# Transposing x by DMA instead of on TensorE, and accumulating two output projections in one PSUM bank

## The chip, the cores and the metric

The kernel runs on one core of one Trainium2 chip. The metric is the device time of one execution in microseconds (us). PE is TensorE (PEld its weight loads), DVE is VectorE, ACT is ScalarE, POOL is GpSimd, SP is the engine that issues the DMAs.

## The reference, cut to what matters

A gated mix of an attention block with a compressive memory (A) and a feed-forward block (B), both on the same 2048 x 512 input x, in bf16:

```python
g = sigmoid((x * gate_w).sum(-1, keepdims=True))      # one gate per row
a = A(x)     # q, k, v projections; 32 heads of 16; 4 segments of 512 rows:
             #   causal softmax attention inside the segment,
             #   plus phi(q) @ M / (phi(q) @ z) from earlier segments; then @ wo
b = (relu(x @ W_gate) * (x @ W_up)) @ W_down          # hidden size 1792
return g * a + (1 - g) * b
```

## The kernel before

The program is a list of tasks for each engine. A small list scheduler in the kernel's own Python, with a duration estimated for each task, puts them in a fixed order per engine and adds semaphore waits. So every edit that changes a dependency or an estimated duration can rebuild the order of all engines.

x is loaded in row layout, transposed on PE (64 transposes of 128 x 128) and copied out of PSUM by DVE:

```python
for c in range(NCH):                       # 4 chunks of 512 rows, loaded into E[c]
    for kt in range(KT):                   # 4
        def f_tr(pe, ...):
            for tt in range(TT):
                pe.transpose(PLb[:, bank, col:col + 128], E[:, e, tt, kt * 128:(kt + 1) * 128], ident[:])
        def f_cp(dv, ...):
            return dv.tensor_copy(xT[:, kt, c * 512:(c + 1) * 512], PLb[:, bank, 0:512])
```

The set-up on GpSimd, in this order: `ident`, `mumask`, memset of `vaug` (4352 bf16 per partition), two small memsets, memset of `wkp` (4096 bf16), then eight strided copies from `wk` into `wkp`. The loads are issued in the order x chunk 0, wq, gate_w, wk, wv, beta, x chunks 1 to 3, then the feed-forward weights.

The output stage of a segment, for each of its four tiles of 128 rows:

```python
# down projection of the hidden tile hT (14 matmuls), evicted by DVE
f_ob: psA  = sum_f hT[f].T @ wd[f]
tmpB:  tmpB = psA * (1 - g) + 0                  # DVE, 512 columns
# attention projection (4 matmuls), evicted by DVE
f_oa: psA' = sum_G oT[G].T @ wo[G]
fin:   osb  = psA' * g + tmpB                    # DVE, 512 columns; then the store
```

The softmax here doesn't subtract the row's maximum and nothing guards it: scores larger than these inputs give would overflow.

## Time and profile before

Median 367.0 us of 4 runs. The engine table of the page of the kernel before (busy us, share of the span, number of instructions):

```profile
## 1 busy us (share of the span) xinstructions
PE 323.3 (88%) x3039; PEld 181.1 (50%) x3072; DVE 230.1 (63%) x581; ACT 216.5 (59%) x275; POOL 94.8 (26%) x149
```

Next, the kernel before by windows. Columns: the stretch, its length, then busy us of each engine with the number of instructions, the mean granted clock of PE (1.00 is full), the DMA share and rate.

```profile
core 0: us, PE busy (x) PEld busy (x) DVE busy (x) ACT busy (x) POOL busy (x), PEclk, DMA share, GB/s
0.00:12.19 12.19, 1.89 (x16) 1.66 (x17) 4.36 (x10) 1.69 (x3) 10.85 (x17) 1.00 0.73 241
...
30.00:60.00 30.00, 25.64 (x256) 10.60 (x258) 24.57 (x59) 22.35 (x24) 9.07 (x14) 0.94 0.23 74
60.00:278.00 218.00, 196.21 (x1980) 99.82 (x2001) 146.82 (x387) 162.49 (x185) 72.05 (x112) 1.00 0.02 6
278.00:345.80 67.80, 66.89 (x563) 52.44 (x564) 34.70 (x79) 21.46 (x56) 0.63 (x1) 1.00 0.03 11
345.80:366.00 20.20, 15.61 (x70) 6.78 (x70) 6.45 (x10) 0.38 (x1) 0.00 (x0) 1.00 0.08 26
```

The attention runs until 278 us with feed-forward matmuls as filler; PE is 90% busy there. (Between 30 and 60 us the clock was 0.94: this run had one stretch at half clock, from 55.34.) From 278 the rest of the feed-forward runs alone and PE is practically full. Before 12.19 us PE does 1.9 us of work. So the kernel is bound by PE's work plus a late start.

The start, in lines of the timeline of the kernel before (start, duration, engine, line, operation, output and inputs, count; in brackets the idle time before and what ended it):

```profile
2.52 3.72 POOL L525 MEMSET vaug<- 128x4352 bf16 x1
...
4.90 1.49 DVE L574 COPY xT<-psL 128x512 bf16<-128x512 bf16 x3 [1.19 <-PE psL L570]
...
11.41 0.31 DVE L540 CAST beta_i<-beta_raw 128x32 f32<-128x32 bf16 x1 [5.02 <-DMA beta_raw<-in_A_beta_dram]
11.63 0.41 DVE L574 COPY xT<-psL 128x512 bf16<-128x512 bf16 x1
...
12.19 3.57 PE L614 MATMUL psA<-xT,wq 128*128 128x512 bf16 x8 [6.05 <-DVE xT L574]
...
25.27 0.40 PE L730 MATMUL psL<-qT,kp 32*128 32x512 bf16 x4
```

DVE copies three of the first four transposed tiles, then stands 5 us for the beta load, then does the fourth; the first projection (L614) follows. The first score matmul (L730) comes at 25.27, after the other transposes.

In the output stage, PE and its weight loads wait for the eviction of the down projection (list of waits; total us, number, longest):

```profile
PEld psA L856 <- DVE tmpB L824: 3.2, 7, 1.3
...
PE psA L856 <- DVE tmpB L824: 1.5, 3, 0.8
```

### The profile page before, as it was taken

How to read it: one execution, taken by the hardware profiler on the slowest of the kernel's cores; microseconds unless marked ns; L12 is line 12 of the kernel's file. 1: busy time of each engine (PE TensorE's matmuls, PEld its weight loads, DVE VectorE, ACT ScalarE, POOL GpSimd, SP SyncE). 2: the span in 40 equal slices, each digit the busy share in tenths (PEclk: the TensorE clock that was granted, in tenths of full speed). 3: DMA queues.
4: the chain of work that ended last, by engine and by line, in shares of the span. 5: the costliest groups of instructions: out<-in, count | busy, mean ns of one | idle time of the engine just before them, and what ended most of it. 6: DMA issues, size and time to landing. Idle time of an engine off the chain costs nothing.

```text
span 365.5 us, 7442 instructions
## 1 busy us (share of the span) xinstructions
PE 323.3 (88%) x3039; PEld 181.1 (50%) x3072; DVE 230.1 (63%) x581; ACT 216.5 (59%) x275; POOL 94.8 (26%) x149
## 2 busy tenths in 40 slices
PE   2698978898899998898899898888998999999995
PEld 1353333354454454443334455555345886488842
DVE  4484898977876656789955548944346543464433
ACT  1337786578887788865665789788554441034400
POOL 8402233233333333333322333333322000000000
PEclk9999998999999999999999999999999999999999
DMA  6960240000000000000000000000000000100001
GB/s 216 365 240 22 69 157 2 0 4 0 2 2 2 0 2 2 3 0 16 0 29 17 1 3 2 1 2 2 14 16 29 3 2 0 36 23 2 3 14 43
DMA packets 10113, 12.27 MB, mean 34 GB/s; under 512 B 1120, under 2 KB 9056, under 8 KB 10080
## 3 DMA queue, kind: packets, MB, share of 16 engines
q1 hardware_dynamic: 10080, 11.81, 9.4%
q8 instruction: 24, 0.39, 0.5%
q14 instruction: 9, 0.07, 0.1%
HBM read 9.71 MB, written 2.10 MB: 32 GB/s over the span
## 4 chain that ended last, share of the span: by engine, by line
PE 60%; DVE 19%; ACT 13%; issue 3%; DMA 2%; SPq 1%; POOL 1%; DVEq 0%; ACTq 0%
PE psA L820 12%; PE psA L788 11%; ACT E L736 11%; PE psA L793 10%; PE psL L730 6%; PE psA L627 5%; PE psA L636 3%; PE psA L749 3%; PE psA L856 3%; DVE amem L687 3%; DMA beta_raw<-in_A_beta_dram 2%; PE psA L614 2%; PE psA L647 2%; DVE kp L630 2%; PE psA L763 1%
## 5 line engine op out<-in xcount | busy, mean ns | idle before, releaser
L736 ACT ACTIVATE E<-psL 128x2048 bf16<-128x2048 f32 (+3 forms) x128 | 158.1, 1235 | 57.0 <-PE psL L730 55.7
L738 POOL TENSOR_SCALAR_AFFINE_SELECT E<-E 128x512 bf16<-128x512 bf16 x128 | 82.4, 644 | 182.7 <-ACT E L736 182.5
L800 DVE TENSOR_TENSOR hT<-psA,rl 128x256 bf16<-128x256 f32 x112 | 47.1, 422 | 51.3 <-ACT rl L799 50.9
L799 ACT ACTIVATE rl<-psA 128x256 bf16<-128x256 f32 x112 | 42.8, 382 | 51.3 <-PE psA L793 27.9
L788 PE MATMUL psA<-xT,wg 128*128 128x256 bf16 x448 | 67.5, 273 | 0.6 <-DMA wg<-in_B_W_gate_dram 0.4
L793 PE MATMUL psA<-xT,wu 128*128 128x256 bf16 x448 | 67.4, 273 | 0.0
L730 PE MATMUL psL<-qT,kp 32*128 32x256 bf16 (+3 forms) x512 | 40.4, 305 | 14.0 <-ACT E L736 13.2
L820 PE MATMUL psA<-wd,hT 128*128 128x512 bf16 x216 | 51.1, 379 | 0.5 <-issue 0.2
L788 PEld LDWEIGHTS psA<-xT,wg 128*128 128x128 bf16 x448 | 40.8, 98 | 10.5 <-issue 2.4
L793 PEld LDWEIGHTS psA<-xT,wu 128*128 128x128 bf16 x448 | 41.9, 98 | 7.8 <-issue 1.0
L730 PEld LDWEIGHTS psL<-qT,kp 32*128 32x128 bf16 x512 | 12.9, 91 | 50.8 <-ACT E L736 38.6
L820 PEld LDWEIGHTS psA<-wd,hT 128*128 128x128 bf16 x224 | 21.0, 98 | 24.1 <-issue 0.8
L627 PE MATMUL psA<-xT,wkp 128*128 128x512 bf16 x120 | 31.4, 391 | 1.4 <-issue 0.9
L757 DVE CAST pvT<-psA 128x512 bf16<-128x512 f32 x32 | 22.0, 688 | 12.7 <-PE psA L749 12.7
L630 DVE CAST kp<-psA 128x512 bf16<-128x512 f32 x32 | 22.0, 687 | 7.9 <-PE psA L627 7.4
L749 PE MATMUL psA<-E,vaug 128*17 128x256 bf16 (+3 forms) x512 | 23.1, 300 | 1.7 <-POOL E L738 0.8
L824 DVE SCALAR_TENSOR_TENSOR tmpB<-psA,omg_all,zero 128x512 bf16<-128x512 f32 x16 | 12.0, 750 | 18.8 <-PE psA L820 18.8
L614 PE MATMUL psA<-xT,wq 128*128 128x512 bf16 x59 | 17.0, 419 | 7.0 <-DVE xT L574 6.0
L861 DVE SCALAR_TENSOR_TENSOR osb<-psA,g_all,tmpB 128x512 bf16<-128x512 f32 x16 | 12.0, 750 | 17.0 <-PE psA L856 17.0
L749 PEld LDWEIGHTS psA<-E,vaug 128*17 128x17 bf16 x512 | 10.2, 89 | 15.5 <-issue 5.1
L856 PE MATMUL psA<-wo,oT 128*128 128x512 bf16 x60 | 15.6, 380 | 2.5 <-DVE tmpB L824 1.5
L627 PEld LDWEIGHTS psA<-xT,wkp 128*128 128x128 bf16 x128 | 11.1, 100 | 13.1 <-issue 2.9
(68 smaller groups left out, 276.8 us busy)
## 6 DMA issues: line engine op xcount, KB each, us to landing
E<-in_A_x_dram SPq DMA_DIRECT2D x4, 512.0 KB
out_dram<-osb SPq DMA_DIRECT2D x16, 128.0 KB
wg<-in_B_W_gate_dram SPq DMA_DIRECT2D x1, 1792.0 KB
wu<-in_B_W_up_dram SPq DMA_DIRECT2D x1, 1792.0 KB
wd<-in_B_W_down_dram SPq DMA_DIRECT2D x1, 1792.0 KB
wq<-in_A_wq_dram SPq DMA_DIRECT2D x1, 512.0 KB
wk<-in_A_wk_dram SPq DMA_DIRECT2D x1, 512.0 KB
wv<-in_A_wv_dram SPq DMA_DIRECT2D x1, 512.0 KB
```

Of the source, the lines that this page charges most:

```text
L627: ins = pe.matmul(A(ep)[:, :], lhsT=wkp[:, kt, n, :], rhs=xT[:, kt, tok0:tok0 + 512], start=(kt == 0), stop=(kt == KT - 1))
L630: dve_t.append(Tk("dve", lambda dv, n=n, ep=ep: dv.tensor_copy(kp16[:, s2, n, :], A(ep)[:, :]), writes=[f"kp16_{s2}_{n}"], dur=c_dve(512), ...
L730: ins = pe.matmul(PL[:, jj, 0:N], lhsT=kp16[32 * jj:32 * jj + 32, s2, n, 128 * j:128 * j + 128], rhs=qT16[32 * jj:32 * jj + 32, s2, G, 128 ...
L736: act_t.append(Tk("act", lambda ac, e=e, N=N: ac.activation(E[:, e, :, 0:N], PL[:, :, 0:N], ACT.Exp, scale=SCALE), reads=[f"bankL{q4}" for ...
L738: pool_t.append(Tk("pool", lambda pl, e=e: pl.affine_select(out=E[:, e, :, 0:128], in_=E[:, e, :, 0:128], compare_op=ALU.is_ge, fill=0.0, ...
L749: ins = pe.matmul(A(epv)[32 * jj:32 * jj + 17, 128 * j:512], lhsT=vaug[:, s2, j, h, :], rhs=E[:, es[j], jj, 0:N], start=(j == 0), stop=(j ...
L788: ins = pe.matmul(A(ep)[:, 0:256], lhsT=wg[:, kt, f * 128:(f + 1) * 128], rhs=xT[:, kt, t0:t0 + 256], start=(kt == 0), stop=(kt == KT - 1))
L793: ins = pe.matmul(A(ep)[:, 256:512], lhsT=wu[:, kt, f * 128:(f + 1) * 128], rhs=xT[:, kt, t0:t0 + 256], start=(kt == 0), stop=(kt == KT - 1))
L799: act_t.append(Tk("act", lambda ac, ep=ep, r=r: ac.activation(rl[:, r, :], A(ep)[:, 0:256], ACT.Relu), writes=[f"rl{r}"], dur=c_act(256), ...
L800: dve_t.append(Tk("dve", lambda dv, ep=ep, r=r, f=f, half=half: dv.tensor_tensor(hT[:, f, half * 256:(half + 1) * 256], A(ep)[:, 256:512], ...
L820: ins = pe.matmul(A(ep)[:, :], lhsT=hT[:, f, i * 128:(i + 1) * 128], rhs=wd[:, f, :], start=(f == 0), stop=(f == NF - 1))
L856: ins = pe.matmul(A(ep)[:, :], lhsT=oT[:, G, i * 128:(i + 1) * 128], rhs=wo[:, G, :], start=(G == 0), stop=(G == 3))
```

## The change

Its intent: take the transposes off PE and the copies off DVE by loading x with transposing DMAs, start earlier, and save the tmpB evictions by letting the two output projections accumulate into one bank. With z the gate's logit, g = e^z (1 - g). So the attention rows are multiplied by e^z where they are normalised anyway, the down projection accumulates on top, and one eviction multiplies the sum by (1 - g).

The core of the diff (renamings, the same dependency per tile in many places, a dependency of every first matmul on the clearing of the PSUM banks, and a longer estimate for the load of wu are cut):

```diff
-            self.now[e] = start + 700.0
+            spb = 1300.0 if task.name.startswith("ldxT") else 700.0      # scheduler's estimate of an issue
+            self.now[e] = start + spb
...
+    def xT_dmas(c):
+        for kt in range(KT):
+            srcx = A_x[0, c * 512:(c + 1) * 512, kt * 128:(kt + 1) * 128]
+            dma(lambda sp, ...: sp.dma_start_transpose(xT[:, kt, c * 512:(c + 1) * 512], srcx), writes=[f"xT{c}_{kt}"], ...)
+    # order of loads: beta, wq, wk, x chunk 0 (4 transposes), gate_w, wv, x chunks 1-3 (12), wg, wu, wo, wd
...
     pool_setup: ident
+                wkp memset, 8 wkp copies, vaug memset          # moved up
                 mumask, zero32, zero512
-                (before: mumask, vaug memset, zero32, zero512, wkp memset, 8 wkp copies)
...
-    (64 PE transposes xtr{c}_{kt} and 16 DVE copies xcp{c}_{kt})
...
-    g_all = sigmoid(z);  omg_all = 1 - g_all
+    omg_all = sigmoid(-z);  gexp = exp(z)
...
-    amem = num * rec                        # tensor_tensor
+    amem = (num * gexp) * rec               # scalar_tensor_tensor
+    rdg  = rden * gexp                      # 32 small multiplies
-    adot = pv * rden
+    adot = pv * rdg
...
+            pe_out.append(Tk("pe", f_oa, reads=[oT..., "wo"] + [f"hT{f}" for f in range(NF)], ...))   # 4 matmuls, stop=False
+            (f_ob: 14 matmuls onto the same bank, start=False, in two halves of 7)
-            tmpB = psA * omg_all;   osb = psA' * g_all + tmpB
+            osb  = psA * omg_all
```

## The prediction

> **What bounds the kernel now.** The engine table of the page: PE 323.3 of 365.5 us (88%), DVE 230, ACT 217; clock 0.995. The chain of waits is 60% PE. By windows, PE's 42 us of idle lie in four places: 10.3 us before the first projection starts at 12.19; some 27 us scattered through the attention part (30 to 280); 0.2 from 280 to 350, where the feed-forward part runs back to back; 4.6 after. So: PE-bound, with a late start.
>
> The start, from the timeline: the 64 PE transposes of x take about 6.9 us of PE (16 take 1.7 in the chain), all before 25 us, with 16 DVE copies of 416 ns (6.5 us). After three of the first four copies (6.4 us) DVE stands for the beta load, issued late (3.48, landed 11.39); the fourth copy, hence the first projection, comes only at 12.0. The first score matmul runs at 25.3.
>
> **What the change does.**
> 1. x arrives transposed by 16 DMAs of 128 KB. PE loses 6.9 us of work, DVE 6.5.
> 2. Beta, wq and wk go first, so that DVE stall is gone; but the first projection needs four transposing DMAs. Plain issues take 0.44 to 0.89 us of the SP queue; the diff's scheduler charges 1.3 us for a transpose. Three issues (1.9 us) plus four at 1.3, from 0.8, end near 7.9; with about 2 us to land I estimate the first projection at 10 to 11. The Trainium skill ("DMA: Bandwidth & Descriptors", section "Latency and other measured facts") gives 261 GB/s for a DMA transpose with a non-contiguous middle dimension: an estimate of 2 us for the first 512 KB, 8 us for all x, less than the issuing (16 x 1.3 = 21 us). No trace shows one yet.
> 3. wg and wu land about 10 us later (wg lands at 20.4 now). Almost no feed-forward runs before 60 us, so this should cost nothing.
> 4. The down projection accumulates onto the attention projection in one PSUM bank. 16 tmpB evictions (750 ns, 12.0 us) leave DVE, and PE's waits for them (4.7 us) go. Added on DVE: 32 small multiplies (16-column ones take 160 to 250 ns: about 7 us) and perhaps 60 ns on each of 48 amem operations (3 us). The first output matmul of a segment now waits for the last hT: about 1.2 us of idle, which at the end eats the saved tmpB step.
>
> **On the critical path.** Transposes 6.9 us and the start 1 to 2 us count nearly in full: attention starts near 16 us instead of 25 and the rest slides forward. The DVE saving is off the path except for 2 to 3 us. The end is a wash. Together 10 to 11 us: **356 us, 349 to 364**. Faster by over 2%: 0.70; within 2%: 0.23; slower: 0.07.
>
> **Signs.** Right: no PE transposes of x in the groups; first projection at 10 to 11 us, first score matmul at 15 to 18; PE busy near 317, DVE near 222; no waits for tmpB; attention ending near 270, then about 85 us of dense feed-forward. Wrong: first projection later than 13 us, or PE standing for a DMA in the gate matmul (which needs all of x) or the first feed-forward block.
>
> **What would make it wrong.** Transposes far slower than 1.3 us each; the rebuilt order filling the attention part better or worse by several us; the added DVE step in the attention chain, where DVE is 95% busy (40 to 60 us).

## The result, and the profile after

Median 359.9 us of 10 runs (359.63 to 361.4) against 366.9 us of 16 runs of the kernel before. The ratio is 0.9822, 95% interval 0.9803 to 0.984: faster by 1.8%, so within 2%. Here and below, a ratio is the mean time of one kernel's runs over that of the other's of the same rounds, so it is not quite the ratio of the medians quoted. Executions over 1.5% slower than the fastest of the same kernel are left out of the means. The time lies in the stated range, but the predicted gain was 10.9 us (366.9 - 356.0) and the measured one is 7.0, and the forecast that had been given 0.70, faster by over 2%, did not come true.

The engine table of the page of the kernel after:

```profile
PE 317.8 (88%) x2974; PEld 175.8 (49%) x3008; DVE 224.0 (62%) x580; ACT 216.0 (60%) x276; POOL 94.3 (26%) x149
```

PE lost 5.5 us of busy time and DVE 6.1, as expected. The windows of the kernel after, cut at the same events:

```profile
0.00:9.28 9.28, 0.00 (x0) 0.03 (x1) 4.28 (x9) 3.03 (x4) 6.10 (x12) 1.00 0.68 171
9.28:30.00 20.72, 18.30 (x81) 6.79 (x83) 14.94 (x31) 8.60 (x9) 8.89 (x14) 0.92 0.67 175
...
60.00:272.40 212.40, 192.44 (x1941) 98.32 (x1967) 143.93 (x387) 159.46 (x182) 69.82 (x110) 0.99 0.03 8
272.40:340.00 67.60, 65.59 (x546) 51.08 (x546) 30.46 (x71) 21.46 (x56) 0.94 (x2) 1.00 0.03 11
```

Two things differ from what was forecast. The clock is lower: 0.92 in the second stretch and 0.99 in the attention part, where the profile before had one dip, 0.94 between 30 and 60 us. And the dense part, where PE was 0.9 us short of full before, is now 2.0 us short (67.60 - 65.59).

The start in the timeline of the kernel after:

```profile
2.26 5.11 SPq L498 DMA_TRANSPOSE xT<-in_A_x_dram  x4
...
9.28 4.90 PE L604 MATMUL psA<-xT,wq 128*128 128x512 bf16 x16 [9.28 <-DMA xT<-in_A_x_dram]
...
10.65 3.72 POOL L534 MEMSET vaug<- 128x4352 bf16 x1
...
11.91 2.76 DVE L610 TENSOR_SCALAR ttmp<-qT 128x512 bf16<-128x512 bf16 x1
...
18.45 0.39 PE L720 MATMUL psL<-qT,kp 32*128 32x512 bf16 x4 [2.09 <-DVE kp L620]
```

The four transposing DMAs take 1.28 us each to issue (5.11 / 4), and the first projection starts at 9.28 us, even earlier than predicted. But the first tensor_scalar on DVE takes 2.76 us; the same operation takes 0.28 later. It ends 0.3 us after the GpSimd memset of vaug does (10.65 + 3.72 = 14.37; 11.91 + 2.76 = 14.67). Everything behind it on DVE is late, PE stands, and the first score matmul comes at 18.45 instead of 15 to 18.

In the output stage the waits for tmpB are gone and new ones are there (waits of PE, kernel after):

```profile
PE psA L827 <- DVE hT L793: 2.6, 2, 1.3
...
PE psA L827 <- DVE mutmp L698: 1.0, 1, 1.0
...
PE psA L827 <- DVE rden L758: 0.3, 1, 0.3
```

L827 is the first output matmul of a segment: it waits for all hidden tiles, twice 1.3 us in front of the dense output stages, and in the attention part for a DVE count that stands behind other DVE work (mutmp, rden).

Finally the clock. The trace's clock records show stretches of exactly 3.41 us at half clock: in the profiled run of the kernel after two of them, from 18.74 and from 148.45. Windows of the kernel after around them:

```profile
145.00:148.45 3.45, 1.59 (x43) 0.83 (x40) 2.14 (x6) 2.09 (x4) 1.76 (x3) 1.00 0.00 0
148.45:151.86 3.41, 3.41 (x41) 1.43 (x41) 1.47 (x3) 1.88 (x1) 0.63 (x1) 0.50 0.01 2
15.00:18.74 3.74, 1.37 (x9) 0.41 (x8) 3.64 (x11) 1.89 (x3) 0.89 (x3) 1.00 0.46 105
18.74:22.15 3.41, 3.41 (x12) 1.19 (x9) 1.96 (x10) 1.88 (x1) 0.65 (x1) 0.50 0.49 112
```

In front of both PE had been busy for less than half the time (1.59 of 3.45 us, 1.37 of 3.74). The Trainium skill ("TensorE: Matmul & The Clock Gate", section "Part 1: The HAM clock gate") describes a gate that halves PE's clock after an idle window, with a window of 3413 ns that runs freely. The length agrees with the records here. But PE was not idle in front of these stretches, and its busy time does not decide either. The profiled run of e4 (below) went to half clock right after this window, with PE busy for 2.72 of 3.41 us, 1.74 of them 64 one-column matmuls of the gate:

```profile
17.90:21.31 3.41, 2.72 (x70) 2.03 (x71) 2.55 (x6) 1.32 (x2) 0.00 (x0) 1.00 1.03 406
```

In e8 and e3, windows with 1.75 and 1.84 us of 3.41 busy (from 17.49 and from 143.82) were followed by none. What sets off a stretch is not settled here.

The clock column needs a caution too: it reads 1.00 also where the trace has no clock record. The first record begins at 17.79 us in the profiled run before and at 11.92 in that after. Until then PE ran at about half clock, as its instructions show: the weight loads of the first projection start 0.43 us apart (before: 12.57, 13.00, 13.42, 13.85), later 0.21 (after: nine in 1.89 us from 11.79). From the first projection on that is 5.6 us before and 2.6 after, so an estimate from these spans is that it cost the run before 1.5 us more (half of the difference). The first record falls elsewhere in other profiled runs (12.37 in e1, 15.26 in e5), so whether the change has a part in it is not shown.

Such a stretch costs time, and the number of them differs from run to run of one kernel. It shows in the granted clock listed with every run: 1.0 or 0.999 for none, 0.994 or 0.995 for one, 0.990 or 0.991 for two (read from the traces where there is one). The runs by that grade:

| kernel | none | one | two |
|---|---|---|---|
| before (rounds of e1 to e4) | 365.6 to 366.5, 9 runs | 367.9, 368.3 | - |
| after | - | 359.6 to 359.9, 7 runs | 361.2 to 361.4, 4 runs |
| e1 | 356.0 to 356.6, 4 runs | 358.7 | 359.9 |
| e2 | 354.8 to 355.3, 5 runs | 356.7 | - |
| e3 | 358.8 | 360.2 to 360.5, 4 runs | 361.9 |
| e5 | 352.8 to 353.4, 4 runs | 355.5, 355.6 | - |

(Two runs of before at 0.997, of which no trace is kept, are counted with none by their times.) One stretch costs 1.2 to 2.5 us between the medians of neighbouring columns, and comparisons finer than that are made below within one column, though some columns hold a single run. Over all rounds before has eleven runs at 0.995 (367.2 to 368.3, median 367.6). Against the seven of after with one stretch the gain is 7.8 us, where the medians of all runs give 7.0.

### The profile page after: what moved, and what is told of

It is laid out like the page before. It is cut to its first block, busy times and chain, and to the rows that moved or that the text cites. A ratio compares the mean times of both kernels' runs of the same rounds, so it can differ in the third digit from the quotient of the medians.

```text
span 359.5 us, 7318 instructions
## 1 busy us (share of the span) xinstructions
PE 317.8 (88%) x2974; PEld 175.8 (49%) x3008; DVE 224.0 (62%) x580; ACT 216.0 (60%) x276; POOL 94.3 (26%) x149
## 4 chain that ended last, share of the span: by engine, by line
PE 53%; DVE 23%; ACT 16%; issue 4%; SPq 1%; DMA 1%; POOL 0%; DVEq 0%; ACTq 0%
PE psA L835 14%; ACT E L726 10%; PE psL L720 7%; PE psA L781 7%; DVE hT L793 6%; ACT rl L792 5%; PE psA L617 5%; PE psA L786 4%; PE psA L739 4%; PE psA L626 4%; PE psA L827 3%; DVE amem L677 3%; DVE kp L620 2%; DVE qT L608 2%; PE psA L753 2%
## 5 line engine op out<-in xcount | busy, mean ns | idle before, releaser
L781 PE MATMUL psA<-xT,wg 128*128 128x256 bf16 x448 | 67.5, 273 | 0.1
L781 PEld LDWEIGHTS psA<-xT,wg 128*128 128x128 bf16 x448 | 41.0, 98 | 10.4 <-issue 2.7
L839 DVE SCALAR_TENSOR_TENSOR osb<-psA,omg_all,zero 128x512 bf16<-128x512 f32 x16 | 12.0, 748 | 35.1 <-PE psA L835 35.1
L617 PE MATMUL psA<-xT,wkp 128*128 128x512 bf16 x120 | 32.3, 397 | 1.7 <-DVE amem L677 0.7
L604 PE MATMUL psA<-xT,wq 128*128 128x512 bf16 x60 | 16.1, 405 | 9.9 <-DMA xT<-in_A_x_dram 9.3
L827 PE MATMUL psA<-wo,oT 128*128 128x512 bf16 x59 | 15.4, 379 | 4.0 <-DVE hT L793 2.6
L677 DVE SCALAR_TENSOR_TENSOR amem<-psA,gexp,ndrec 128x128 bf16<-128x128 f32 x48 | 16.5, 345 | 1.3
```

What stands on the lines that cost most here:

```text
L617: ins = pe.matmul(A(ep)[:, :], lhsT=wkp[:, kt, n, :], rhs=xT[:, kt, tok0:tok0 + 512], start=(kt == 0), stop=(kt == KT - 1))
L677: dve_t.append(Tk("dve", lambda dv, dst=dst, srcn=srcn, bc=bc, t=t: dv.scalar_tensor_tensor(out=dst, in0=srcn(), scalar=gexp[:, t:t + 1], ...
L781: ins = pe.matmul(A(ep)[:, 0:256], lhsT=wg[:, kt, f * 128:(f + 1) * 128], rhs=xT[:, kt, t0:t0 + 256], start=(kt == 0), stop=(kt == KT - 1))
```

## The experiments

All give a correct result. Each was timed in five rounds beside the kernel before on the same chip (six runs each, but five of e6 and four of e8). Differences to the 359.9 us of the kernel after are those of the medians. Taken through the ratios to before (0.9822 for after) they are smaller: 2.5 us for e1, 4.7 for e2, 5.8 for e5.

### e1: the memset of vaug earlier

Theory: the GpSimd memset keeps DVE's first operation on SBUF operands from running. The Trainium skill ("SBUF — State Buffer", section "Who interferes with whom") says that DVE and GpSimd share a pair of SBUF ports under an exclusive lock, that copies, casts and tensor_scalar can take it on the DVE side, and that a DVE operation with at most one SBUF input, outside the modes that use two ports, does not contend. The copies from PSUM in the kernel before agree (413 to 425 ns beside the memset). The edit keeps the order of PE, DVE and ACT the same as after's (compared instruction by instruction), so nothing but the memset's place differs:

```diff
     pool_setup: wkp memset
+                vaug memset (all of it)         # here POOL waits for wk anyway
                 8 wkp copies
-                vaug memset
+                memset of one element of vaug   # keeps the dependencies and the order
```

> The kernel after, with the 3.7 us GpSimd memset of vaug moved ahead of the wkp copies (a one-element memset keeps its old place, so that the order of PE, DVE and ACT is the same as after's). Theory A (that memset holds the SBUF ports that the first DVE tensor_scalar needs): the first tensor_scalar drops from 2.76 us to under 0.8, the first score matmul comes at 15.5 to 16.5 us instead of 18.45, and the total falls by 2 to 4 us, to 356 to 358. Rival B (the late start is given back in the attention part): the first score matmul comes earlier, but the total stays within 1 us of 359.9. Rival C (the long tensor_scalar has another cause): it stays near 2.7 us.

Measured: 356.4 us (6 runs, 356.0 to 359.9), ratio 0.9755 (0.9715 to 0.9794). Two lines of its timeline:

```profile
11.88 0.67 DVE L611 TENSOR_SCALAR ttmp<-qT 128x512 bf16<-128x512 bf16 x1
...
16.51 0.39 PE L721 MATMUL psL<-qT,kp 32*128 32x512 bf16 x4 [0.40 <-DVE kp L621]
```

The tensor_scalar fell from 2.76 to 0.67 us (the small wkp copies still run beside it) and the first score matmul moved from 18.45 to 16.51. Theory A held. The hold is moved, not gone: the memset now lies beside the beta cast, which took 4.87 us (1.19 in after) and ended at 8.68 as the memset did (8.64). There it costs nothing, as DVE then waits for the first projection until 11.15. Of the 3.5 us, only 1.1 to 1.4 are seen between runs with equally many half-clock stretches (358.7 against 359.8; 359.9 against 361.3; one run of e1 each). The rest is that four of six runs had no such stretch, where all eleven of the kernel after had one or two. That is consistent with the profiled run, in which one of them followed directly on the stall (15.00 to 18.74 above), but what decides which run gets one is not settled; that part is argued, not shown.

### e2: no wait for the last hidden tile

Again the same order on all engines. Only the semaphore wait of the first output matmuls on the last hidden tile is left out; they don't read it. The second half of the down projection, which does, keeps its wait.

```diff
+            pe_out[-1].soft = (f"hmul{s}_{NF - 1}_0", f"hmul{s}_{NF - 1}_1")   # ordered after, not waited for
```

> The kernel after in the same order on every engine; only the first output matmul group of a segment no longer waits for the last hidden tile (the second half of the down projection still does, where it is read). Theory A (the two 1.3 us PE waits before the output stage of segments 2 and 3 lie on the path): both vanish and the total falls by 2.3 to 2.9 us, to about 357.3. Rival: the wait only moves to the second half of the down projection, and the total stays within 0.7 us of 359.9.

Measured: 354.95 us (6 runs, 354.8 to 356.7), ratio 0.9694 (0.9669 to 0.972). More than expected. In its timeline the output stage follows without a gap (no bracket):

```profile
294.20 0.81 PE L830 MATMUL psA<-wo,oT 128*128 128x512 bf16 x3
```

Its list of PE's waits has none of the three lines shown for after, so 2.6 + 1.0 + 0.3 = 3.9 us of waits are gone; the expectation had counted only 2.6, the two in the dense part. In runs with one half-clock stretch the difference to after is 3.1 us (356.7, a single run, against 359.8). The rest is again the number of stretches: five of six runs had none. In the kernel after, the wait of 1.0 us lies at 146.7 to 147.8 us, inside the thin stretch before the half clock at 148.45; in the profiled run of e2, PE was busy 2.36 and 3.00 of 3.40 us in the two stretches there, and no half clock followed.

### e3: DVE's saved work put back

```diff
+                if t < 12:      # segments 0 to 2: one more 512-column eviction, to a scratch tile
+                    dv.scalar_tensor_tensor(out=scr[:, t, :], in0=A(ep)[:, :], scalar=omg_all[:, t:t + 1], in1=zero512[:, :], ...)
                 return dv.scalar_tensor_tensor(out=osb[:, r, :], ...)
```

> The kernel after with 12 extra 512-column DVE evictions of 0.75 us (9 us of DVE work), one beside each output eviction of segments 0 to 2, the order otherwise the same. It puts back the load that dropping tmpB took off DVE, without its waits. Theory A (that saving lies off the path): total within 1 us of 359.9. Rival (DVE time in the attention part counts, as the prediction's 2 to 3 us assumed): 3 us or more longer.

Measured: 360.25 us, ratio 0.9832 (0.9803 to 0.986), 0.4 us more than after, and 0.4 us too within the column of one stretch. Nine us of DVE work more cost almost nothing. The DVE time that dropping tmpB saves lies off the critical path.

### e4 and e11: the kernel before with beta issued first

e4 moves one load. e11 adds that the two memsets write the same bytes as fp32, half as many elements, in the same order as e4.

```diff
# e4
+    dma(beta_raw <- A_beta)            # first of all
     for c in range(NCH): ...
-            dma(beta_raw <- A_beta)    # before: sixth
# e11, on top
-    pl.memset(wkp[:], 0.0)
+    pl.memset(wkp[:].bitcast(F32), 0.0)
-    pl.memset(vaug[:], 0.0)
+    pl.memset(vaug_flat[:].bitcast(F32), 0.0)
```

> The kernel before with one edit: the beta load is issued first. Theory A (the start of before is bound by DVE standing for beta): the first projection starts at 7 to 8.5 us instead of 12.19 and the total falls by 2 to 4.5 us, to 362.5 to 365. Rival (the 12.19 is bound by the loads of x or wq): first projection stays later than 10 us and the total within 1 us of 366.9.

> e4 (the kernel before with beta issued first) with the two memsets written as fp32, in the same order as e4. Theory A (in e4 the beta cast on DVE was held for 6.5 us by the two memsets): the cast falls to under 2 us, the first projection comes 3 to 5 us earlier than e4's 18.1, and the total falls by 2 to 4 us to 360 to 362. Rival (e4's start is bound by the other three loads of x, which its order puts first): the cast is short but the first projection stays later than 17, total within 1 us of 364.3.

Measured: e4 364.3 us, ratio 0.9948 (0.9923 to 0.9973); e11 364.1 us, ratio 0.9944. Both expectations failed in part, and e4 shows why its own did. From its timeline:

```profile
2.52 3.72 POOL L525 MEMSET vaug<- 128x4352 bf16 x1
3.75 6.50 DVE L540 CAST beta_i<-beta_raw 128x32 f32<-128x32 bf16 x1
...
6.71 3.51 POOL L528 MEMSET wkp<- 128x4096 bf16 x1
```

Beta was there at 3.75, but the cast of 32 columns took 6.50 us, until 10.25: it was held through the memset of vaug, two small ones, and that of wkp, which ended at 10.22. Removing the wait for the load had only uncovered a second one. In e11 the cast takes 2.98 us and ends at 6.74, again as the (shorter) memset of wkp ends (6.71). So the hold is real. Yet the first projection stays at 17.6 us against 18.1 in e4, and the total does not move, as the rival said: the rebuilt order puts all 64 transposes in front of the first projection, so the loads of the later chunks set its time (PE stands 5.45 us for one until 12.60). Both runs together show that the reordered load by itself, with the order rebuilt around it, was worth 2 us.

### e5 and e9: both mends

e5 is e1 and e2 together, e9 adds the fp32 memsets; both in the same order as after on PE, DVE and ACT.

> The kernel after with both mends of the first two runs (vaug memset early, no wait for the last hidden tile), in the same order on PE, DVE and ACT. If the two are separate waits, their gains add: 359.9 - 3.5 - 4.9 = 351.5 us; part of each may be the same half-clock window, counted twice, so 351 to 353.5. If they hide each other: 355 or more.

> Both mends (as e5), and the two long GpSimd memsets (wkp, vaug) write the same bytes as fp32, half the elements; the order on PE, DVE and ACT is the same as after's. If a memset costs per element, each falls from 3.5 and 3.7 us to about 1.8 and 1.9, both end near 5.2 us, before DVE has work from SBUF: beta cast 0.3 us, first tensor_scalar 0.3. Total 352 to 353.5 us, at most 1 us below e5, since in e5 the first tensor_scalar was already short. If a memset costs per byte, they stay as they are and the total equals e5.

Measured: e5 353.2 us (352.8 to 355.6), ratio 0.9663 (0.9635 to 0.969); e9 354.1 us (352.7 to 355.7), ratio 0.9667. Within the column of one half-clock stretch the gains add: 1.1 for e1, 3.1 for e2, 4.3 for e5 (355.5 against 359.8). The medians add less (3.5 and 4.9 against 6.7), since both mends remove half-clock stretches and a stretch can be removed only once. e9 equals e5: its lower runs are 352.7 to 353.2, but three of its six had a stretch, so its median missed the 352 to 353.5 expected. In e9 the memsets behave as a cost per element says:

```profile
1.47 1.80 POOL L532 MEMSET wkp<- 128x2048 f32 x1
...
3.21 1.91 POOL L533 MEMSET vaug<- 128x2176 f32 x1
```

They had taken 3.51 and 3.72 us. e5 and e9 are the fastest kernels, 3.3 to 3.4% below the kernel before.

### e6, e7 and e12: the change in halves

e6 is the kernel before with the input half (DMA transposes, order of loads, order of GpSimd's set-up); e7 is the kernel before with the output half (gate folded into the attention rows, one accumulation). Their diffs are the matching parts of the one above. Their orders are rebuilt by the scheduler. e12 is e6 with the fp32 memsets, in e6's order.

> The kernel before with only the input half of the change: DMA transposes, the new order of loads and of GpSimd's set-up work; the output stage with tmpB stays. Theory A (the gain is the 6.9 us of PE transposes and the earlier start): 358 to 361 us, first score matmul near 18 us with the first tensor_scalar again near 2.7 us. Rival (the fused output stage brings the gain): 364 or more.

> The kernel before with only the output half of the change: gate folded into the attention rows, one accumulation for both projections; x is still transposed on PE with the loads and set-up as before. Theory A: the waits for tmpB (4.7 us on PE and its weight loads) are exchanged for waits for the last hidden tile (3.9 us), so 364 to 367.5 us. Rival (the fused stage brings the gain): 362 or less.

> e6 (the input half alone, output stage with tmpB as before) with the two memsets written as fp32, in the same order as e6. It takes the same hold off the start as e1, so it should fall from e6's 357.7 by 2 to 3.5 us. Theory A (the fused output stage, once its wait for the last hidden tile is gone, is worth 1 us or more): 354 to 355.7 us, against 352.7 to 353.2 of the mended fused kernel in its runs at full clock. Rival (the fused stage is worth nothing even then): 353.2 or less.

Measured: e6 357.7 us, ratio 0.9787 (0.9762 to 0.9812). e7 366.1 us, ratio 0.9995 (0.9973 to 1.0016). e12 356.7 us, ratio 0.9717 (0.9692 to 0.9742). The input half brings the whole gain and is by itself as fast as the whole change (359.5 and 359.7 against 359.6 to 359.9 in runs with one stretch). As expected its first tensor_scalar took 2.81 us and its first score matmul came at 18.50. The output half brings nothing: e7 has no waits for tmpB, and 4.3 us of PE waits for the last hidden tile in their place. e12 missed its expectation (354 to 355.7; 2 to 3.5 us below e6): it is only 1.0 us below e6 by the medians, which agrees with the 1.1 of e1 between like runs; e6 had few half-clock stretches to lose. Against e5 and e9 in their runs without a stretch (352.7 to 353.4) e12, which had none in all its runs (356.4 to 356.9), is 3.5 us slower, so the fused output stage is worth about that much, order included, once its wait is mended.

### e8 and e10: the first 512 rows of x through PE

Since SP issues a transpose in 1.28 us, the first chunk could be there sooner by one plain load and 16 PE transposes. e8 does that on top of both mends, with the sigmoid of beta reading the bf16 row itself; e10 adds the fp32 memsets in e8's order.

```diff
-    xT_dmas(0)
+    dma(E[0] <- x chunk 0)        # second load, after beta; then 16 PE transposes and 4 DVE copies as before
```

> Both mends, and the first 512 rows of x come by one plain load and 16 PE transposes instead of four DMA transposes (the other 1536 rows stay with the DMA); the beta cast is dropped, the sigmoid reads the bf16 row itself. The order is rebuilt. Theory: the start of after is bound by the four transposing issues of 1.28 us each on the SP queue, so the first projection moves from 9.28 to 7 to 8 us and the first score matmul to 14 to 15.5, and the total to 348.5 to 352 us. Rival (start is bound by wq or by GpSimd's wkp): first score matmul not before 16, total not below that of both mends alone.

> e8 with the two memsets written as fp32, in the same order on PE, DVE and ACT. Theory A (in e8 the DVE set-up operations from SBUF were held until the memset of wkp ended at 8.65 us, and the x copies stood behind them): the set-up scale operation falls from 3.88 us to under 0.6, the first projection comes at 7 to 8 us instead of 10.94, the first score matmul at 15.5 to 17 instead of 19.5, and the total falls by 2 to 4 us to 353 to 355. Rival (wq's load or the copies bound it): first projection not before 10 us, total 356 to 357.

Measured: e8 356.9 us, ratio 0.9747 (0.9727 to 0.9767); e10 356.6 us, ratio 0.9744. In e8 the hold struck a third time:

```profile
4.80 3.88 DVE L562 TENSOR_SCALAR epsv<-romgh 128x32 f32<-128x32 f32 x1
5.13 3.52 POOL L532 MEMSET wkp<- 128x4096 bf16 x1
```

A set-up operation of 0.17 us took 3.88, until the memset ended at 8.65, and the x copies stood behind it; the first projection started at 10.94. With that e8's expectation failed: its four runs, none with a stretch, are 3.5 us or more above e5's without one. In e10 the operation took 0.38 us and the first projection started at 7.81, as expected; but the first score matmul came at 17.1, no sooner than e1's 16.5. PE had begun the key projection at 13.11 (e1: 14.23), without waiting for wkp, whose copies ended at 12.13. What it then waited for, 2.10 us, was DVE: in the rebuilt order DVE makes all four query features before it copies the first key tile, at 16.35 (e1: 15.77). The total did not fall as expected: all six runs of e10 had one or two half-clock stretches. Within the column of one, e10 has 355.8 us against 354.9 to 355.7 for e9. The earlier first projection buys nothing here.

## Why the prediction was right or wrong, point by point

- **PE-bound, and the transposes count.** Right. The input half alone gave 8.4 us (366.15 to 357.74) where the prediction had 6.9 for the transposes plus 1 to 2 for the start. In part that is luck: the first score matmul moved by 6.8 us (25.27 to 18.50 in e6), not by the 9 that the step below assumes, so some 1.6 us of the 8.4 came from elsewhere, the rebuilt order or the clock at the start; no run separates these. PE busy came to 317.8 (said: near 317), DVE to 224.0 (near 222).
- **The cost of transposing DMAs.** Right, and slightly better than said: 1.28 us per issue, the last of the first four landed about 1.9 us after its issue ended (7.37), the first projection at 9.28 instead of 10 to 11. The skill's 261 GB/s is not tested by any run: 128 KB per 1.28 us is 102 GB/s, so the issuing sets the pace at which x arrives, as predicted. PE waited for it once, at the start.
- **The later feed-forward weights cost nothing.** Right: the gate's first feed-forward matmuls wait for no DMA in the profile after (idle before L781: 0.1 us).
- **"Attention starts near 16 us instead of 25 and the rest slides forward".** This step failed. It came at 18.45. The prediction read that DVE's stall for beta went away, and did not ask what else the moved memset of vaug would now run beside. That memset held a DVE tensor_scalar for 2.5 us; e1 takes it away (16.51) and is 1.1 us faster between like runs, 3.5 in the medians.
- **"Added on DVE ..."** Right in size: 32 multiplies of 203 ns (6.5 us; said about 7), 58 ns on each amem operation (345 against 287; said 60).
- **"The DVE saving is off the path except for 2 to 3 us".** Too much: putting 9 us back cost 0.4 us (e3). The 4.7 us of "PE's waits" were too much as well: they add PE's own (1.5) to those of its weight loads (3.2), which run beside PE's work.
- **"The first output matmul of a segment now waits ... about 1.2 us of idle, which at the end eats the saved tmpB step".** The mechanism was right, and the end is a wash: from the last feed-forward matmul to the end 19.7 us before (345.8 to 365.5) and 19.8 after (339.7 to 359.5). The term was mis-sized: it was counted once, and it occurs in every segment, 3.9 us in the profile. e2 takes it away and gains 3.1 us between like runs, 4.9 in the medians.
- **What was not in the sum at all:** the half-clock stretches. The eleven runs of the kernel after all had one or two, those of before in the rounds of e1 to e4 mostly none (its profiled run had one), and e1, e2 and e5 mostly lost them again. Between runs with one stretch each the gain is 7.8 us, so they account for about 0.8 of the 3.9 us by which the gain fell short. Why the kernel after met them in every run and e1 in two of six is not settled.

So the expected 10 to 11 us became 7: the input half gave the sum that was said for it, though attention started later than said, and of the output terms the gain was near 0 (e7), with the new wait in place of the old one.

## What to carry to other kernels

When a change moves a long GpSimd operation, look at what DVE will do beside it: here an operation of 0.17 us from SBUF to SBUF was held for 3.88 us, until the memset ended, and a cast for 6.50 as another memset followed, while DVE copies from PSUM kept their 413 to 425 ns. A wait that is attached to a whole group of matmuls should be put on the first one that reads the data; in this kernel, where PE is the bound, taking out 3.9 us of such waits gave 3.1 us between like runs. And when testing parts of a change in a kernel whose order is generated, make the variants in the same order, and compare runs at the same granted clock, or a difference of one or two microseconds says nothing here, where one half-clock stretch costs 1.2 to 2.5.

## What the Trainium skill lacked or had wrong

- "SBUF — State Buffer", section "Who interferes with whom": the hold itself agrees (2.76 us for a tensor_scalar of 0.28; 3.88 for one of 0.17). The page says that whoever issues first has the ports for the whole instruction. It does not say that a DVE operation which already waits can lose to the next GpSimd instructions too: in e4 a cast waited from 3.75 us through the memset that ended at 6.24 and also through the ones after it, until 10.25. The same is seen in e1 (3.81 to 8.68), e8 (4.80 to 8.68) and e11 (3.76 to 6.74).
- "GPSIMD Engine Reference": no cost of a GpSimd memset is given. Here it goes by elements, not bytes: 3.51 us for 4096 bf16 per partition, 1.80 us for the same bytes as 2048 fp32; 3.72 and 1.91 for 4352 and 2176.
- "DMA: Bandwidth & Descriptors": the page gives the sequencer's cycles for a DMA transpose of small tiles from HBM and for a large one inside SBUF, but no issue time for one of this size from HBM. Here one of 512 x 128 bf16 took 1.28 us on SP, against 0.39 to 0.58 us for the plain loads beside it, and the issuing, at 102 GB/s, set the pace.
- "TensorE: Matmul & The Clock Gate", section "Part 1: The HAM clock gate": the window's length agrees (3.41 us). The page's table has the half clock come after an idle window, and its text gives no busy share below which one comes; here PE was still busy for 37% to 46% of the 3.4 to 3.7 us before a half-clock stretch in the kernel after, for 61% (2.07 of 3.41) in the kernel before, and for 80% (2.72 of 3.41) in e4, while 51% (1.75, e8) and 54% (1.84, e3) were followed by none. Each stretch cost 1.2 to 2.5 us, and the count changed from run to run.
